# Who makes the low parts of the split weights: Pool's share moved to DVE in a Trainium2 expert-and-mixing kernel

## The chip, the core and the metric

The kernel runs on one core of one Trainium2 chip. The core has five queues of work: PE (the TensorE matmuls; its weight loads are listed apart as PEld), DVE (VectorE), ACT (ScalarE), POOL (GpSimd, called Pool here) and SP (SyncE, which issues transfers). The metric is the device time of the core in microseconds (us). Before the change it is 706.55 us, the median of three runs (706.11 to 706.99).

## The reference

Three layers follow one another on float32 arrays: a windowed attention, a mixture of experts in which each token goes to one of eight experts, and a gated mixing over the sequence (its weights come as float64).

```python
# attention: 4 batches, 8 heads, 576 tokens, 64 dims; plain or dilated window mask
attn = softmax(where(mask, q @ k.T / 8, -1e9));  x = attn @ v          # -> (4, 576, 512)
# experts: e = argmax of the token's logits, or the expert of the token before
h = np.maximum(x[b, s] @ w1[e], 0.0)                                    # w1[e]: 512 x 1024
out[b, s] = p[e] * (h @ w2[e])                                          # w2[e]: 1024 x 512
# gated mixing
h = np.maximum(x @ w_in, 0.0);  u, v = halves of h
gated = u * (w_spatial @ normalised(v) + b_spatial)
y = gated @ w_out
```

## The kernel before

**Split products.** A float32 product of the expert and mixing stages is made of three TensorE products of operands in the fp32r format: high by high, high by low, low by high. So every operand is split. `split` (line 548) first has ACT copy the source into the high part (line 549) and then another engine subtract the high part from the source, which gives the low part (line 550). Its last argument names that engine; without it, it is DVE.

**Experts.** After the attention (about the first 180 us of the trace) tokens of one expert are worked in blocks of 128 rows, block after block in one row. `block(j)` (line 1157) lets PE do the first layer of block j+1 (`stage1`, lines 999 to 1001, reading `w1h`, `w1l`, `xh`, `xl`), turn the rows of block j+2 (line 976), do the second layer of block j (`stage2`, lines 1033 to 1035, reading `w2h`, `w2l`, `hh`, `hl`), and turn the hidden rows of block j+1 (line 1012). In between, the next operands are made: `divide(1, j+2)` splits the w1 of block j+2 from the buffer `raw1` into `w1h`, `w1l` after stage 1 has read the old ones; `turn_x` makes `xh` (ACT, line 984) and `xl` (DVE, line 985); `divide(2, j+1)` splits w2 from `raw2`; `turn_h` makes `hh` (ACT, line 1022) and `hl` (DVE, line 1023). `divide` (line 950) works in four pieces of 128 x 1024; piece c = 1 is given to Pool, pieces 0, 2 and 3 to DVE. It runs under a condition, since consecutive blocks of one expert keep the weights; the tests and jumps of that condition have line 958.

**Mixing weights.** In twelve of the blocks `narrow` (line 1055) turns a piece of the float64 weights into float32 with five DVE steps (lines 1065 to 1071) and one of ACT, all in the buffer `scratch`. It returns the split of the result, which runs one block later (`rest.pop()()`, line 1192); that split gives the low part (`wil`, `wol`, 128 x 512) to Pool.

**Order.** Each engine takes its instructions in the order in which the code issues them. On DVE a block's order is: low parts of w1 if the expert changes, `xl`, low parts of w2 if the expert changes, `hl` twice, the five steps of `narrow`, and the copy of the next row list `ix` (line 970). On Pool it is: the gather of the rows of a later block (line 972, an indirect transfer), its piece of w1, its piece of the mixing weights, its piece of w2. SP fetches the next raw weights piece by piece (line 569) as soon as the piece in the buffer has been read.

Of the kernel before, what the change touches and what calls it, by code (L numbers as in the profile page):

```python
# [18 lines left out]
ET = mybir.EngineType  # L19
# [50 lines left out]
def moe_stack(ctx: ExitStack, tc: tile.TileContext, q, k, v, w_gate, w_local, w1, w2, w_in, w_sp, b_sp, w_out, out):  # L70
    nc = tc.nc
# [8 lines left out]

    # ---------------------------------------------------------------- constants
    warm = const.tile([128, 512], BF16, name="warm")
# [38 lines left out]

    # ---------------------------------------------------------------- routing state
    idxacc = rt.tile([128, NCOL], F32, name="idxacc")
    slot_i = rt.tile([128, LB], I32, name="slot_i")
    sel_all = rt.tile([128, LB, E], F32, name="sel_all")
    # of each token: its block among its expert's blocks, its row in it, and its weight
    trips = rt.tile([128, LB, 3], F32, name="trips")
# [7 lines left out]
    def steps(f):  # L135
        """A closure's parts, between which other work may come."""
        g = f()
        if g is not None:
            yield from g
# [9 lines left out]
    def router(b, xT, pieces, sides, bank):  # L149
        """Adds the closures that route batch b to stages."""  # L150
        st = {}
# [93 lines left out]
        def scan3():  # L245
            sv = st["sv"]
            if b == 0:
                # How many blocks of each expert hold tokens of the first batch.
                ci = rt2.tile([E, 2], I32, name="ci")
                nc.vector.tensor_scalar(out=ci[:, 0:1], in0=state["cum"], scalar1=127.0, scalar2=None, op0=ALU.add)  # L250
                nc.vector.tensor_scalar(out=ci[:, 1:2], in0=ci[:, 0:1], scalar1=7, scalar2=None, op0=ALU.arith_shift_right)
                state["first"] = rt.tile([E, 1], F32, name="first")
                nc.vector.tensor_copy(state["first"], ci[:, 1:2])
            nc.scalar.activation(sv[:, S:640], sv[:, 512:S].bitcast(F32), AF.Copy)
# [134 lines left out]
        def rows():  # L389
# [18 lines left out]
            if b < 3:  # L408
                return
            # The block before which every row of the first batch is there, if there is such a one.  # L410
            it = iota128[0:1, 0:n]
# [17 lines left out]
        def after():  # L429
            """Where this list's blocks of each expert begin, how many they are, and where the next list begins."""  # L430
            sf, en, nb, (j0, j1) = st["sf"], st["en"], st["nb"], LISTS[b]
            D = state["D"]
            base = rt2.tile([E, 1], F32, name="base")
            if b == 1:
                nc.vector.tensor_copy(base, sf)
            else:
                nc.vector.tensor_scalar(out=base, in0=sf, scalar1=state["got"], scalar2=float(j0), op0=ALU.subtract, op1=ALU.add)
            nc.vector.tensor_scalar(out=D[:, 2 * b - 2], in0=ident[0:E, 0:E], scalar1=base, scalar2=None, op0=ALU.mult)
            yield
            if b == 3:  # L440
                return
            n = j1 - j0
            tk = rt2.tile([E, 1], F32, name="tk")
            nc.vector.tensor_scalar(out=tk, in0=sf, scalar1=-1.0, scalar2=float(n), op0=ALU.mult, op1=ALU.add)
            yield
            nc.vector.tensor_scalar(out=tk, in0=tk, scalar1=0.0, scalar2=nb, op0=ALU.max, op1=ALU.min)
            yield
            got = rt.tile([E, 1], F32, name=f"got{b}")
            if b == 1:
                nc.vector.tensor_copy(got, tk)  # L450
            else:
                nc.vector.tensor_add(got, state["got"], tk)
            nc.vector.tensor_scalar(out=D[:, 2 * b - 1], in0=ident[0:E, 0:E], scalar1=got, scalar2=None, op0=ALU.mult)
            yield
            last = rt2.tile([E, 1], F32, name="last")
            nc.vector.tensor_scalar(out=last, in0=sf, scalar1=float(n), scalar2=None, op0=ALU.is_lt)
            yield
            l2 = rt2.tile([E, 1], F32, name="l2")
            nc.vector.tensor_scalar(out=l2, in0=en, scalar1=float(n), scalar2=None, op0=ALU.is_ge)
            yield  # L460
            nc.vector.tensor_mul(last, last, l2)
            yield
            st["last"], st["new"] = last, got
# [75 lines left out]
    stages = []  # L539
    state["bank"] = R()  # L540

    # ---------------------------------------------------------------- attention
    sc = ctx.enter_context(tc.tile_pool(name="sc", bufs=1))
# [11 lines left out]
    def fetch1(j, i):  # L555
        """The first two blocks have their own copies of w1, the first one also of w2, and use them as they are."""
        e = value(1, j, [ET.SP], E - 1)
# [24 lines left out]
    def attention(aw, ap, qkp, plan):  # L582
# [13 lines left out]
        npair = B * 4  # L596
        # A head's keys fill half of the rows and meet zeros in the other half, which lets the products use both heads' queries as they lie.
        kz = [[aw.tile([128, S], F32, name=f"kz{p}{hh}", bufs=1) for hh in range(2)] for p in range(2)]
# [4 lines left out]
        def load_qk(u):  # L603
            b, pr = divmod(u, 4)
            n, c = (96, 6) if pr < 2 else (72, 8)
            for w_, src in ((0, q), (1, k)):
                t = qkp.tile([96, 1024], F32, name=f"qk{w_}", bufs=3)
                if w_:
                    # Keys come head by head, each partition's tokens in one piece.
                    tv = t[0:n, 0:2 * c * D].rearrange("p (h m) -> p h m", h=2)  # L610
# [52 lines left out]
        def T_k(u, hh, tag="T"):  # L663
            """Turns a head's keys two neighbours at a time, whose dimensions then lie in the two halves of the rows."""
            def f():
# [172 lines left out]
        def feed(i):  # L838
            """Parts of the routing, as many as a step can take along; the tensor engine gets one only when its operands had time to be made."""
            nonlocal budget  # L840
# [83 lines left out]

    # ---------------------------------------------------------------- experts
    aps, aws, qks, w1s, mws, mps, xps = [ExitStack() for _ in range(7)]
# [23 lines left out]
    def divide(which, j, always=False):  # L950
        def parts():
            for c in range(4):
                split(*halves(which, c), nc.gpsimd if c == 1 else nc.vector)
        if always:
            parts()
            return
        ch = value(3, j, [ET.Activation, ET.DVE, ET.Pool], 1)
        with tc.If(ch > 0):  # L958
            parts()

    def own(key, pool, shape, dt, tag=None):
        """A tile that stays for all blocks."""
        if key not in P:
# [91 lines left out]
    def narrow(c):  # L1055
        """A piece of the float64 weights as float32, and that in two parts."""
        if c < 8:
# [13 lines left out]
        nc.vector.scalar_tensor_tensor(out=mf, in0=mf, scalar=2.0 ** -20, in1=sc.bitcast(F32), op0=ALU.mult, op1=ALU.mult)  # L1071
        return lambda: split(hi_, lo_, mf, nc.gpsimd)

    def early(kind, c=0):
        """The steps of blocks 0 and 1 that run beside the last of the attention."""
        def bankT():
# [22 lines left out]
    def pop(kind="any"):  # L1099
        """The next step of the routing; "pe": if the tensor engine has a part in it; "rest": all up to such a one."""  # L1100
        while stages and (kind == "any" or (kind == "pe") == hasattr(stages[0], "on_pe")):
# [4 lines left out]
    def ahead(what, j, must=False):  # L1106
        """Issues the gathers or fetches up to block j that the lists already give."""
        while done[what] <= min(j, NBLK - 1):
# [35 lines left out]
    def gate(j, engines=None):  # L1144
        """Blocks that every count of tokens fills run straight, the others where they hold any."""
        if j < SURE:
# [70 lines left out]
    rest = []  # L1217
# [9 lines left out]

    # ---------------------------------------------------------------- gated mixing over the sequence
    gr = ctx.enter_context(tc.tile_pool(name="gr", bufs=1, side="right", reuse_waits="tile"))
# [11 lines left out]
    def mixing(gw):  # L1241
# [17 lines left out]
        def turn_w(si):  # L1259
            """A part of the weights over the sequence, turned; the last 64 columns twice, for the two places of a batch's last tokens."""  # L1260
            w2x = G["w2x"]
# [61 lines left out]
        def norm3(g):  # L1323
            vr, _ = vn[g]
            if g % 9 == 4:
                # The last 64 tokens of two batches: a batch's high parts and, in the other half, its low parts.
                for t, a, z in ((tails[0], slice(0, 64), slice(64, 128)), (tails[1], slice(64, 128), slice(0, 64))):
# [59 lines left out]
        def project(b, gh, gl):  # L1387
# [3 lines left out]
            for ah, al, i in items:  # L1391
                o = gw.tile([128, C], F32, name="o", bufs=2)
                # The very last piece in two halves, so that less of it is left at the end.
                for cs in [slice(0, C)] if (b, i) != (B - 1, 3) else [slice(0, 256), slice(256, C)]:
# [86 lines left out]
```

## Time and profile before

| what | value |
|---|---|
| median of the runs | 706.55 us (706.11 to 706.99) |
| profiled execution: span from the first to the last instruction | 705.2 us |
| what the median has beside that span | 1.35 us |
| PE busy over the span | 672.2 us (95%) |
| DVE, ACT, POOL busy over the span | 423.9, 386.0, 194.2 us |

The median is 1.35 us above the profiled span; this is taken as what lies around the span. A PE that is listed as busy is not PE at its peak: a matmul's record is longer than the distance to the next one, since they are pipelined. What a row of the trace says is: start in us, length in us, engine, line, operation, the tile written <- the tiles read, shapes, how many merged, and in brackets the engine's idle time before it with what ended that idle time.

### The profile page before, as it was taken

How to read it: one execution, taken by the hardware profiler on the slowest of the kernel's cores; microseconds unless marked ns; L12 is line 12 of the kernel's file. 1: busy time of each engine (PE TensorE's matmuls, PEld its weight loads, DVE VectorE, ACT ScalarE, POOL GpSimd, SP SyncE). 2: the span in 40 equal slices, each digit the busy share in tenths (PEclk: the TensorE clock that was granted, in tenths of full speed). 3: DMA queues.
4: the chain of work that ended last, by engine and by line, in shares of the span. 5: the costliest groups of instructions: out<-in, count | busy, mean ns of one | idle time of the engine just before them, and what ended most of it. 6: DMA issues, size and time to landing. Idle time of an engine off the chain costs nothing. (4 is left out here: it accounts for less than half of the span.)

```text
span 705.2 us, 14287 instructions
## 1 busy us (share of the span) xinstructions
PE 672.2 (95%) x4395; PEld 571.1 (81%) x4396; DVE 423.9 (60%) x1379; ACT 386.0 (55%) x780; POOL 194.2 (28%) x226
## 2 busy tenths in 40 slices
PE   8999898989999999999999999897999999999998
PEld 6989797885478788787788877775898998998997
DVE  4667869777966747877866656342664164154151
ACT  5788777653635646666665556333735336335322
POOL 6443434341424405425424254112010110000000
PEclk9999999999999999999999999999999999999999
DMA  6776545594446776586556746415110220200102
GB/s 152 180 174 152 129 118 131 189 347 126 138 150 204 249 283 231 199 314 213 192 195 223 283 142 233 165 32 162 30 46 0 76 60 1 75 16 1 60 2 74
DMA packets 90644, 101.36 MB, mean 144 GB/s; under 512 B 49984, under 2 KB 60992, under 8 KB 90560
## 3 DMA queue, kind: packets, MB, share of 16 engines
q1 hardware_dynamic: 87120, 89.10, 39.7%
q0 software_dynamic: 3440, 11.27, 5.0%
q8 instruction: 36, 0.59, 0.3%
q14 instruction: 48, 0.39, 0.2%
HBM read 139.68 MB, written 17.30 MB: 223 GB/s over the span
## 5 line engine op out<-in xcount | busy, mean ns | idle before, releaser
L1001 PE MATMUL hp<-w1h,xl 128*128 128x512 f32 x168 | 66.9, 398 | 7.0 <-DVEq L958 6.1
L1033 PE MATMUL yp<-w2h,hh 128*128 128x512 f32 x176 | 71.6, 407 | 0.2 <-ACT hh L1022 0.2
L1035 PE MATMUL yp<-w2h,hl 128*128 128x512 f32 x176 | 69.9, 397 | 1.7 <-DVE hl L1023 1.7
L972 POOL DMA_INDIRECT xs<-x_d,ix x25 | 30.8, 1232 | 144.7 <-PE xTp L976 56.1
L1034 PE MATMUL yp<-w2l,hh 128*128 128x512 f32 x176 | 69.6, 395 | 0.0
L743 POOL TENSOR_TENSOR ms<-ms,mxa 96x384 f32<-96x384 f32 (+2 forms) x64 | 51.1, 799 | 64.9 <-DVE mxa L740 39.7
L999 PE MATMUL hp<-w1h,xh 128*128 128x512 f32 x168 | 68.4, 407 | 0.2 <-issue 0.2
L1000 PE MATMUL hp<-w1l,xh 128*128 128x512 f32 x168 | 66.4, 395 | 0.0
L740 DVE CUSTOM_DVE_ANT_0 ms<-S,masks 96x128 f32<-96x128 f32 (+2 forms) x224 | 54.4, 249 | 16.8 <-PE S L729 8.2
L550 DVE TENSOR_TENSOR w2l<-raw,w2h 128x1024 fp32r<-128x1024 f32 x30 | 48.7, 1649 | 24.5 <-ACT w2h L549 24.2
L550 DVE TENSOR_TENSOR w1l<-raw,w1h 128x1024 fp32r<-128x1024 f32 x30 | 55.7, 1902 | 5.3 <-ACT w1h L549 4.6
L729 PE MATMUL S<-kz,qT 128*96 128x128 f32 (+2 forms) x448 | 53.2, 259 | 0.4 <-POOL vt L632 0.4
L1151 POOL DMA_INDIRECT yg<-y_d,slot_i x14 | 13.4, 958 | 138.5 <-PE tr L1283 102.6
L776 PE MATMUL PV<-vt,ptS 128*96 128x65 f32 (+2 forms) x448 | 44.4, 240 | 7.0 <-issue 2.9
L1023 DVE TENSOR_TENSOR hl<-hTp,hh 128x512 fp32r<-128x512 f32 x44 | 30.3, 689 | 33.9 <-ACT hh L1022 31.9
L1022 ACT ACTIVATE hh<-hTp 128x512 fp32r<-128x512 f32 x44 | 26.2, 596 | 43.6 <-DVE hl L1023 38.2
L776 PEld LDWEIGHTS PV<-vt,ptS 128*96 128x96 f32 (+2 forms) x448 | 38.7, 156 | 9.7 <-issue 3.6
L729 PEld LDWEIGHTS S<-kz,qT 128*72 128x72 f32 (+1 forms) x448 | 45.4, 155 | 1.2 <-POOL vt L626 0.9
L1001 PEld LDWEIGHTS hp<-w1h,xl 128*128 128x128 f32 x168 | 31.5, 188 | 17.1 <-DVEq L958 8.4
L549 ACT ACTIVATE w2h<-raw 128x1024 fp32r<-128x1024 f32 x40 | 41.1, 1060 | 6.0 <-PE yp L1035 3.4
L549 ACT ACTIVATE gtiles<-gt 128x288 fp32r<-128x288 f32 (+2 forms) x48 | 15.7, 359 | 48.0 <-DVE gt L1377 48.0
L1035 PEld LDWEIGHTS yp<-w2h,hl 128*128 128x128 f32 x176 | 33.1, 188 | 10.7 <-DVE hl L1023 3.0
(309 smaller groups left out, 1825.5 us busy)
## 6 DMA issues: line engine op xcount, KB each, us to landing
raw<-in_moe_w SPq DMA_DIRECT2D x188, 512.0 KB
y_d<-y SPq DMA_DIRECT2D x30, 256.0 KB
qk<-in_q SPq DMA_DIRECT2D x32, 144.0 KB
qk<-in_k SPq DMA_DIRECT2D x32, 144.0 KB
x_d<-xo SPq DMA_DIRECT2D x32, 144.0 KB
scratch<-in_moe_w_in SPq DMA_DIRECT2D x8, 512.0 KB
out<-o SPq DMA_DIRECT2D x15, 256.0 KB
vt<-in_v SPq DMA_DIRECT2D x48, 64.0 KB
```

The lines of the kernel that those rows point to most:

```text
L549: nc.scalar.activation(dst_h, src, AF.Copy)
L550: (eng or nc.vector).tensor_tensor(out=dst_l, in0=src, in1=dst_h.bitcast(F32), op=ALU.subtract)
L729: nc.tensor.matmul(ps[0:nq, j, 0:nk], l, r, start=True, stop=True)
L740: nc.vector.tensor_tensor_reduce(out=ms[0:nq, j, 0:nk], in0=ps[0:nq, j, 0:nk], in1=masks[0:nq, m, 0:nk], scale=-0.125, scalar=3.0e38, op0= ...
L743: nc.gpsimd.tensor_tensor(out=ms[0:nq, 0:nb, 0:nk], in0=ms[0:nq, 0:nb, 0:nk], in1=mx[0:nq, 0:nb].unsqueeze(2).to_broadcast([nq, nb, nk]), ...
L776: nc.tensor.matmul(ops[0:nq, j], ptS[0:nk, j, 0:nq], r, start=True, stop=True)
L999: nc.tensor.matmul(ps[n], xh[:, kk], wh[:, kk, cs], start=(kk == 0), stop=False)
L1000: nc.tensor.matmul(ps[n], xh[:, kk], wl[:, kk, cs], start=False, stop=False)
L1001: nc.tensor.matmul(ps[n], xl[:, kk], wh[:, kk, cs], start=False, stop=(kk == 3))
L1033: nc.tensor.matmul(ps, hh[:, f], P["w2h"][:, f], start=(f == 0), stop=False)
L1034: nc.tensor.matmul(ps, hh[:, f], P["w2l"][:, f], start=False, stop=False)
L1035: nc.tensor.matmul(ps, hl[:, f], P["w2h"][:, f], start=False, stop=(f == 7))
```

## The change

The engine argument is gone from both calls, so DVE makes all low parts, and Pool drops out of the engines that read the condition of `divide`. Comments and docstrings were also dropped, which makes no instruction.

```diff
     def divide(which, j, always=False):
         def parts():
             for c in range(4):
-                split(*halves(which, c), nc.gpsimd if c == 1 else nc.vector)
+                split(*halves(which, c))
         if always:
             parts()
             return
-        ch = value(3, j, [ET.Activation, ET.DVE, ET.Pool], 1)
+        ch = value(3, j, [ET.Activation, ET.DVE], 1)
         with tc.If(ch > 0):
             parts()
...
-        return lambda: split(hi_, lo_, mf, nc.gpsimd)
+        return lambda: split(hi_, lo_, mf)
```

On DVE, at a block whose expert changes (`raw_3652` is the buffer of the raw w1), the difference of the two orders is:

```order
 L553 TENSOR_LOAD rowi
 L958 COMPARE_AND_BRANCH
-L550 TENSOR_TENSOR w1l<-raw_3652,w1h 128x1024 x3
+L550 TENSOR_TENSOR w1l<-raw_3652,w1h 128x1024 x4
 L958 UNCONDITIONAL_BRANCH x2
 L985 TENSOR_TENSOR xl<-xTp,xh 128x512
```

A fourth piece stands in DVE's row ahead of `xl`, between the same neighbours. The low part of a piece of the mixing weights stands on DVE after the change behind `xl` and ahead of the low parts of w2 (`raw_141` is the buffer of the raw w2):

```order
L550 TENSOR_TENSOR w1l<-raw_3652,w1h 128x1024 x4
L958 UNCONDITIONAL_BRANCH x2
L985 TENSOR_TENSOR xl<-xTp,xh 128x512
L550 TENSOR_TENSOR wil<-scratch,wih 128x512
L553 TENSOR_LOAD rowi
L958 COMPARE_AND_BRANCH
L550 TENSOR_TENSOR w2l<-raw_141,w2h 128x1024 x4
```

Before, `wil` was not in DVE's row, and the two splits had three pieces each. On Pool, in the same blocks, before the change (`xs_...` are the gathered rows, `ix_...` the row lists):

```order
L972 DMA xs_3097<-x_d,ix_2925 128x512
L553 TENSOR_LOAD rowi
L958 COMPARE_AND_BRANCH
L550 TENSOR_TENSOR w1l<-raw_3652,w1h 128x1024
L958 UNCONDITIONAL_BRANCH x2
L550 TENSOR_TENSOR wil<-scratch,wih 128x512
```

And after the change, from the same gather on:

```order
L972 DMA xs_3097<-x_d,ix_2925 128x512
L958 UNCONDITIONAL_BRANCH x2
L972 DMA xs_2927<-x_d,ix_3095 128x512
L958 UNCONDITIONAL_BRANCH x2
L972 DMA xs_3097<-x_d,ix_3687 128x512
```

Pool's row there holds only the gathers and the jumps.

## Rows read from the trace of the kernel before

**Rows 1.** The page: the span.
```profile
span 705.2 us, 14287 instructions
```
**Rows 2.** Busy time by stretch: experts, then mixing; last three: PEclk, DMA share, GB/s.
```profile
180.00:476.00 296.00, 285.98 (x1347) 225.87 (x1345) 197.18 (x274) 165.26 (x241) 106.79 (x69) 1.00 0.57 201
476.00:705.20 229.20, 221.78 (x1375) 202.05 (x1373) 95.03 (x246) 94.72 (x243) 14.58 (x16) 1.00 0.15 47
```
**Rows 3.** Groups by line, 180 to 476 us: busy, mean ns, idle before, releasers.
```profile
L1035 PE MATMUL yp<-w2h,hl 128*128 128x512 f32 x176 | 69.9, 397 | 1.7 <-DVE hl L1023 1.7
...
L1001 PE MATMUL hp<-w1h,xl 128*128 128x512 f32 x168 | 66.9, 398 | 7.0 <-DVEq L958 6.1 <-DVE xl L985 0.9
...
L550 DVE TENSOR_TENSOR w1l<-raw,w1h 128x1024 fp32r<-128x1024 f32 x30 | 55.7, 1902 | 5.3 <-ACT w1h L549 4.6 <-DMA y_d<-y 0.7
L550 DVE TENSOR_TENSOR w2l<-raw,w2h 128x1024 fp32r<-128x1024 f32 x29 | 47.4, 1663 | 24.5 <-ACT w2h L549 24.2 <-DVE xl L985 0.2
...
L550 POOL TENSOR_TENSOR w1l<-raw,w1h 128x1024 fp32r<-128x1024 f32 x10 | 25.7, 2571 | 0.2
```
**Rows 4.** Timeline of PE around the wait at 297 us.
```profile
296.49 0.40 PE L1000 MATMUL hp<-w1l,xh 128*128 128x512 f32 x1
297.89 0.50 PE L1001 MATMUL hp<-w1h,xl 128*128 128x512 f32 x1 [1.00 <-DVEq L958]
298.22 0.40 PE L999 MATMUL hp<-w1h,xh 128*128 128x512 f32 x1
298.46 0.40 PE L1000 MATMUL hp<-w1l,xh 128*128 128x512 f32 x1
```
**Rows 5.** Timeline of PE: the first matmul after other such waits.
```profile
234.07 0.50 PE L1001 MATMUL hp<-w1h,xl 128*128 128x512 f32 x1 [0.90 <-DVE xl L985]
...
433.86 0.50 PE L1035 MATMUL yp<-w2h,hl 128*128 128x512 f32 x1 [0.85 <-DVE hl L1023]
...
443.19 0.50 PE L1001 MATMUL hp<-w1h,xl 128*128 128x512 f32 x1 [2.16 <-DVEq L958]
...
462.82 0.50 PE L1035 MATMUL yp<-w2h,hl 128*128 128x512 f32 x1 [0.82 <-DVE hl L1023]
```
**Rows 6.** Timeline of DVE, 291 to 298 us (the x3 row and its third piece).
```profile
291.53 5.71 DVE L550 TENSOR_TENSOR w1l<-raw,w1h 128x1024 fp32r<-128x1024 f32 x3 [0.42 <-ACT w1h L549]
...
293.81 3.43 DVE L550 TENSOR_TENSOR w1l<-raw,w1h 128x1024 fp32r<-128x1024 f32 x1
297.16 0.68 DVE L985 TENSOR_TENSOR xl<-xTp,xh 128x512 fp32r<-128x512 f32 x1
```
**Rows 7.** Timeline of POOL over the same stretch.
```profile
291.85 1.75 POOL L972 DMA_INDIRECT xs<-x_d,ix  x1 [7.91 <-PE yp L1035]
293.62 2.54 POOL L550 TENSOR_TENSOR w1l<-raw,w1h 128x1024 fp32r<-128x1024 f32 x1
296.12 2.25 POOL L550 TENSOR_TENSOR wil<-scratch,wih 128x512 fp32r<-128x512 f32 x1
```
**Rows 8.** Timeline of ACT over the same stretch.
```profile
289.22 3.91 ACT L549 ACTIVATE w1h<-raw 128x1024 fp32r<-128x1024 f32 x4
...
293.99 0.59 ACT L984 ACTIVATE xh<-xTp 128x512 fp32r<-128x512 f32 x1
```
**Rows 9.** Timeline of DVE at 188 us, where POOL has no work.
```profile
188.18 3.50 DVE L550 TENSOR_TENSOR w1l<-raw,w1h 128x1024 fp32r<-128x1024 f32 x3
```
**Rows 10.** Timeline of DVE before the waits at 433 and 443 us.
```profile
429.39 3.82 DVE L550 TENSOR_TENSOR w2l<-raw,w2h 128x1024 fp32r<-128x1024 f32 x2 [0.68 <-ACT w2h L549]
...
435.84 1.22 DVE L550 TENSOR_TENSOR w1l<-raw,w1h 128x1024 fp32r<-128x1024 f32 x1 [0.45 <-ACT w1h L549]
437.56 4.97 DVE L550 TENSOR_TENSOR w1l<-raw,w1h 128x1024 fp32r<-128x1024 f32 x2 [0.50 <-ACT w1h L549]
```
**Rows 11.** Timeline of PE: the turn of the rows gathered at 291.85 us.
```profile
303.13 0.60 PE L976 MATMUL xTp<-ident,xs 128*128 128x128 f32 x4
```
**Rows 12.** The tile of gathered rows: time from issue to landing.
```profile
DMA to landing us min/median/max: 3.4/4.2/6.6
```

## The prediction

> **What bounds the kernel now.** I read the stretches first: where is PE not busy, and at which clock does it run? From 180 us on, the granted clock is 1.00 (the upper of the two levels, 2.4 GHz), in the expert stage as in the mixing stage [rows 2]. In the expert stage PE is listed busy for 285.98 of 296.00 us, DVE for 197.18 and POOL for 106.79; in the mixing stage POOL has 14.58 us of work in all. So the change can act in the expert stage only, and there PE is the bound, apart from about 10 us.
>
> Next come the groups by line of that stage. The reader is to look at the idle time in front of each PE group. Two groups carry nearly all of it: line 1001, which needs `xl`, waits 7.0 us, and line 1035, which needs `hl`, waits 1.7 us; both waits are ended by DVE [rows 3]. Where the releaser is called DVEq L958, it is the jump at the end of the condition around the split: `xl` comes right behind it. These 8.7 us are eight waits: one is shown in full [rows 4], four more by the matmul that ends them [rows 5], and three repeat the first at 324.16, 350.43 and 414.20 us with 0.97, 0.98 and 0.97 us of idle time. A matmul's record is 0.40 us long while the next starts 0.24 us later (298.22 to 298.46), and here 1.40 us lie between 296.49 and 297.89 [rows 4]. A wait therefore costs its idle time plus 0.16 us: 8.65 + 8 x 0.16 = 9.9 us in all.
>
> Last, the timelines of DVE, POOL and ACT in front of one such wait, to see why DVE is late. DVE needs 5.71 us for three pieces of w1, from 291.53 to 297.24; its third piece alone is on record for 3.43 us from 293.81 on [rows 6]. At 188 us, where POOL has nothing to do, three such pieces take 3.50 us [rows 9]. It isn't ACT that holds DVE up: ACT has all four high parts done at 289.22 + 3.91 = 293.13 us, before DVE begins its third piece [rows 8]. POOL is at its own piece from 293.62 to 296.16 [rows 7], and DVE's third piece ends 1.08 us behind that, which is about the time of one piece alone. Then POOL's piece of `wil` begins at 296.12 and needs 2.25 us, to 298.37, that is 1.13 us past the end of DVE's piece. The two engines take turns, a whole instruction at a time; while POOL is at its piece, DVE stands still.
>
> The page SBUF — State Buffer of the Trainium skill says so as a rule (section "SBUF: two separate sides"): VectorE and GpSimd have a pair of ports in common, an exclusive lock for a whole instruction, and a VectorE operation with two SBUF inputs contends for it with a GpSimd operation that reads SBUF. By that rule a piece given to POOL saves DVE nothing. This case's trace agrees (3.43 us for the piece in POOL's way).
>
> **The change part by part.**
>
> *A piece on DVE.* From rows 9 with one record of 1.22 us [rows 10]: (3.50 - 1.22) / 2 = 1.14 us from piece to piece, so four take 3.50 + 1.14 = 4.64 us. POOL needs 2.57 us for one on average [rows 3].
>
> *The w1 splits ahead of a wait.* Where DVE works through without a gap, as at 291.53, three pieces in POOL's way took 5.71 us and four alone take 4.64: `xl` comes 1.07 us earlier. Four waits are of this kind, costing 1.16, 1.13, 1.14 and 1.13 us, so each keeps at most 0.1 us: 4.2 us are gained. The w2 splits one block earlier become shorter too, so DVE may start these sooner and the rest goes as well: 4.5 us; I take 4.35.
>
> At 437.56 two pieces take 4.97 us behind an idle 0.50 us [rows 10]. Alone, two take 3.50 - 1.14 = 2.36; the new piece fills the gap and adds 1.14 - 0.50 = 0.64. So `xl` comes 4.97 - 2.36 - 0.64 = 1.97 us earlier, of a wait of 2.16 + 0.16 = 2.32 us: 1.97 gained, 0.35 left. The wait that ends at 234.07 has the same pattern ahead of it and costs 1.06 us: all gained.
>
> *The w2 splits ahead of a wait.* At 429.39 two pieces take 3.82 us behind a gap of 0.68 us [rows 10]: 3.82 - 2.36 - (1.14 - 0.68) = 1.00 us earlier, against 0.85 + 0.16 = 1.01. The one at 462.82 is alike (0.82 + 0.16 = 0.98). Gained: 1.98 us.
>
> *The other splits.* Of 20 splits 12 have no wait behind them. They change DVE's queue alone, and in the same direction, since 30 pieces of w1 took 55.7 us [rows 3] while 40 alone take some 40 x 1.14 = 46 us. No gain on PE is counted for them.
>
> *The mixing weights.* DVE gets twelve pieces of 128 x 512. Nearest row: `xl`, of the same size, 0.68 us [rows 6]. They stand behind `xl`, so PE's next need of `xl` isn't touched; behind them wait the low parts of w2 and `hl`, which DVE now reaches about 1 us earlier anyway. I take 0 for them; if that cover were gone at each of the twelve, 12 x 0.68 = 8.2 us would be the upper end. The operand `mf` was read by POOL and is now read by DVE itself, so the next step of `narrow` waits for nobody.
>
> *What leaves POOL.* Its tests of the condition, one per split, with no wait of PE behind them: 0. POOL's gathers no longer queue behind splits. SP fetches the next raw piece when the piece before is read; piece 1 is now read by DVE as its second and not by POOL at 296.16 us [rows 7], so transfers start earlier, on queues that are busy 0.57 of the time [rows 2]: 0.
>
> Sum: 4.35 + 1.97 + 1.06 + 1.98 = 9.4 us. The span goes from 705.2 [rows 1] to 695.8 us; the median of the runs lies 1.35 us above the span, so 706.55 - 9.4 = 697.1 us.
>
> **The rivals.**
>
> *DVE becomes the bound (slower).* DVE is the engine PE waits for, and it gets 32 instructions more. If the 3.43 us were not POOL's doing, but came from something that stays, each split would take one piece longer, 1.14 us. The place is the row w1 pieces, `xl`, line 1001 (and w2 pieces, `hl`, line 1035); each of the eight waits would grow by 1.14: 9.1 us, 715.7 us, and up to 8.2 more if `wil` got into the way too. It decides from the point on which a fourth piece costs more than the stretch that goes, 5.71 - 3.50 = 2.21 us. For it: only one row shows three pieces without POOL. Against: DVE and POOL end one behind the other twice within 3 us [rows 6, 7]. 5%.
>
> *The gathers starve.* The gather at 291.85 stays on POOL for 1.75 us beside DVE's pieces [rows 7]; it may be held up by them, as POOL's `wil` is. With four pieces in a row and POOL shut out until the last, at 291.53 + 4.64 = 296.17, the rows would land by 296.17 + 6.6 = 302.8 us at worst [rows 12]; PE turned them at 303.13 [rows 11], and would do so 1.16 us earlier, at 301.97. That makes up to 0.8 us at each of ten w1 splits, 8 us given back: 705 us. Against: the gather did end at 293.60 in the middle of DVE's row of pieces, and the median landing is 4.2 us [rows 12]. 4%. [...]
>
> *Half of it.* PE, once it no longer waits for `xl`, meets something else close behind: `xh` of ACT (done at 294.58, against a need of `xl` at 296.7, [rows 8]), a raw piece that lands late, or the twelve new instructions ahead of `hl`. Then 3 to 7 us stay, 699.5 to 703.5 us. For it: most of these waits are only 1 us, so a small delay elsewhere eats much of one. Against: 2 us of room on ACT. 15%.
>
> *Nothing moves.* The gaps are hidden by a wait later in the stage, up to the last block, whose y rows the mixing stage gathers. Against: the mixing stage begins with PE's own last products, which move along. 706.5 us, 4%.
>
> **How the numbers follow.** The forecast, 8.5 to 10.3 us gained (696.2 to 698.1), has 72%: the upper end takes all 9.9 us of waits and some 0.4 of a run's spread. Of the rivals 28% are left, half of it in the partial gain. The range 695.8 to 703 holds the forecast and nearly all of the partial one, some 85%. A difference of 0.2%, 1.4 us, is about what a measurement of this kernel can tell from none. Faster: 72 + 15 + most of the gathers' case = 90%; same: 4%; slower: 6%.
>
> **What would show it.** POOL with no split in the expert stage; the w1 pieces of DVE at 1.2 us each with none above 2 us, 40 of them in less than the 55.7 us that 30 took; the waits in front of line 1001 at about 0.3 to 0.8 us in all and those of line 1035 gone. It is wrong if the pieces of DVE stay long without POOL, if the waits are back with another releaser (a transfer, ACT), or if line 976 begins to wait for `xs`.

## The result, and the profile after

The changed kernel takes 695.46 us (median of four runs, 694.24 to 699.27), the kernel before in the same comparison 706.77 us (706.11 to 710.61). The ratio is 0.9839, 95% interval 0.9803 to 0.9874. Forecast were 697.1 us and a range of 695.8 to 703.0: the direction, the place and the mechanism hold, the gain is larger than forecast, and the time lies 0.3 us below the range.

The profiled execution is shorter by 705.2 - 694.2 = 11.0 us. First the page's span and, from the busy times by stretch, the expert stage and what follows it (length; then PE, PEld, DVE, ACT, POOL; then granted clock, DMA share, GB/s). These lines answer to [rows 1, 2]:

```profile
span 694.2 us, 14124 instructions
```
```profile
180.00:465.00 285.00, 283.12 (x1345) 226.19 (x1344) 192.47 (x303) 164.46 (x240) 34.81 (x37) 1.00 0.59 208
465.00:694.20 229.20, 222.62 (x1376) 203.60 (x1374) 95.56 (x246) 94.63 (x243) 14.56 (x16) 0.99 0.15 46
```

The stretches are cut where the last product of line 1035 starts, to a whole us (475.94 us before, 465.20 after). In the first of them PE is idle for 1.9 us in place of 10.0. From that last product to the end of the span there are 229.3 us before and 229.0 after (705.2 - 475.94 and 694.2 - 465.20). DVE is busy for 192.47 us in the first stretch, less than the 197.18 before, although it does 29 instructions more there; POOL falls from 106.79 to 34.81 us.

The groups by line of the same stretch (busy, mean ns, idle before, releasers) answer to [rows 3]:

```profile
L1033 PE MATMUL yp<-w2h,hh 128*128 128x512 f32 x176 | 71.7, 407 | 0.5 <-ACT hh L1022 0.5
...
L1035 PE MATMUL yp<-w2h,hl 128*128 128x512 f32 x175 | 69.4, 397 | 0.0
L1001 PE MATMUL hp<-w1h,xl 128*128 128x512 f32 x168 | 66.5, 396 | 0.1
L550 DVE TENSOR_TENSOR w1l<-raw,w1h 128x1024 fp32r<-128x1024 f32 x40 | 46.4, 1223 | 4.1 <-ACT w1h L549 3.3 <-DMA y_d<-y 0.8
L550 DVE TENSOR_TENSOR w2l<-raw,w2h 128x1024 fp32r<-128x1024 f32 x38 | 45.7, 1224 | 14.8 <-ACT w2h L549 14.5 <-DMA raw<-in_moe_w 0.2
```

Forty pieces of w1 take 46.4 us where thirty took 55.7, and no piece is long any more. In the view of line 550 (instructions by operation, ns min/median/max) the spread of the forty is:

```profile
L550 DVE TENSOR_TENSOR w1l<-raw,w1h x40: 1211/1220/1325, 185.5 to 431.4; 128x1024 fp32r<-128x1024 f32 x40
```

The same block as in [rows 4, 6, 7], on DVE, POOL and PE:

```profile
289.00 4.63 DVE L550 TENSOR_TENSOR w1l<-raw,w1h 128x1024 fp32r<-128x1024 f32 x4 [0.42 <-ACT w1h L549]
293.55 0.68 DVE L985 TENSOR_TENSOR xl<-xTp,xh 128x512 fp32r<-128x512 f32 x1
294.15 0.68 DVE L550 TENSOR_TENSOR wil<-scratch,wih 128x512 fp32r<-128x512 f32 x1
```
```profile
289.32 1.73 POOL L972 DMA_INDIRECT xs<-x_d,ix  x1 [12.21 <-DVE ix L970]
```
```profile
294.70 0.40 PE L1000 MATMUL hp<-w1l,xh 128*128 128x512 f32 x1
294.94 0.39 PE L1001 MATMUL hp<-w1h,xl 128*128 128x512 f32 x1
295.17 0.40 PE L999 MATMUL hp<-w1h,xh 128*128 128x512 f32 x1
```

Four pieces need 4.63 us (4.64 forecast), `xl` is done at 294.23, 0.7 us ahead of PE, and PE starts a product every 0.24 us. Of the eight waits one is left, where 0.35 us were forecast to stay [rows 5, 10]: 0.50 us between two starts, 0.27 more than usual.

```profile
432.73 0.40 PE L1000 MATMUL hp<-w1l,xh 128*128 128x512 f32 x1
433.23 0.50 PE L1001 MATMUL hp<-w1h,xl 128*128 128x512 f32 x1
433.56 0.39 PE L999 MATMUL hp<-w1h,xh 128*128 128x512 f32 x1
```

The gathers land as they did before. In the first profile of the kernel before, only 3 of the 25 gathers have a landing on record, and [rows 12] is made of these three. With all 25 on record the same view reads, in the changed kernel and in a second profile of the kernel before (`before_again`, below):

```profile
DMA to landing us min/median/max: 3.3/5.6/8.0
```
```profile
DMA to landing us min/median/max: 3.4/5.4/7.7
```

PE waits for a gather once in this stage, ahead of the first turn of rows, for 0.72 us before and 0.84 us after.

### The profile page after: what moved, and what is told of

It reads as the page before. It is cut to its first block, busy times and chain, and to the rows that moved or that the text cites. A ratio compares the mean times of both kernels' runs of the same rounds, so it can differ in the third digit from the quotient of the medians.

```text
span 694.2 us, 14124 instructions
## 1 busy us (share of the span) xinstructions
PE 669.7 (96%) x4395; PEld 571.9 (82%) x4396; DVE 420.4 (61%) x1411; ACT 385.3 (56%) x780; POOL 122.8 (18%) x194
## 5 line engine op out<-in xcount | busy, mean ns | idle before, releaser
L550 DVE TENSOR_TENSOR w1l<-raw,w1h 128x1024 fp32r<-128x1024 f32 x40 | 46.4, 1223 | 4.1 <-ACT w1h L549 3.3
L549 ACT ACTIVATE w1h<-raw 128x1024 fp32r<-128x1024 f32 x40 | 39.3, 1048 | 1.8 <-ACT w1h L549 1.0
L1033 PEld LDWEIGHTS yp<-w2h,hh 128*128 128x128 f32 x176 | 33.2, 188 | 7.5 <-ACT hh L1022 0.7
```

The lines of the kernel that those rows point to most:

```text
L549: nc.scalar.activation(dst_h, src, AF.Copy)
L550: (eng or nc.vector).tensor_tensor(out=dst_l, in0=src, in1=dst_h.bitcast(F32), op=ALU.subtract)
L1033: nc.tensor.matmul(ps, hh[:, f], P["w2h"][:, f], start=(f == 0), stop=False)
```

## The experiments

The figure compared below is the length of the expert stage, from PE's first turn of rows at about 183 us (line 976) to the start of its last product of line 1035. It takes out what the attention and the mixing differ by from run to run. Before: 475.94 - 183.68 = 292.26 us; after: 465.20 - 183.06 = 282.14 us; gain 10.1 us. The first and the last line before, then after:

```profile
183.68 0.66 PE L976 MATMUL xTp<-ident,xs 128*128 128x128 f32 x4 [0.72 <-DMA xs<-x_d,ix]
...
475.94 0.40 PE L1035 MATMUL yp<-w2h,hl 128*128 128x512 f32 x1
```
```profile
183.06 0.66 PE L976 MATMUL xTp<-ident,xs 128*128 128x128 f32 x4 [0.84 <-DMA xs<-x_d,ix]
...
465.20 0.40 PE L1035 MATMUL yp<-w2h,hl 128*128 128x512 f32 x1
```

The cost of a wait is given here as the distance between the starts of the two products around it, less the usual 0.235 us.

**Both kernels once more** (no edit).

> The changed kernel once more, for the size of the gain and the spread of its runs. Theory A (the eight waits of the expert stage are gone, each was dearer than its idle time plus 0.16 us; the rest of the 11 us is what differs from run to run in the stretches at the lower clock): 10 us of the gain lie between PE's turn of rows at 183 us and the last product of the expert stage in every profile, and the total scatters by some us with the granted clock (0.990 to 0.997); ratio 0.983 to 0.988. Theory B (part of the gain is made in the attention, 0.6 us before 183 us, by the changed kernel): that 0.6 us is there again.

Measured: 695.58 us (seven runs, 694.21 to 698.81), ratio 0.9813 (0.9783 to 0.9842), a little below the 0.983 to 0.988 expected. Expert stage 282.13 us. PE's first turn of rows comes at 186.27 us, in place of 183.06: theory B fell, the 0.6 us of the first pair are scatter.

> The kernel before, profiled a second time. Theory A: the eight waits stand at the same places with the same length within 0.1 us, the expert stage takes 292.3 us from the turn of rows at 183 us to its last product, and the stretches at the lower clock lie elsewhere than at 120 and 150 us, so the attention ends up to 0.7 us earlier or later. Theory B: the attention ends at the same time as in the first profile within 0.1 us.

Measured: 705.51 us (one run); expert stage 292.61 us, with the same eight waits (1.08, 1.13, 1.14, 1.13, 1.12, 0.98, 2.31, 0.98 us); first turn of rows at 182.40 us, with the lower clock at 82 and 122 us in place of 120 and 152. As theory A has it.

**The two halves of the change apart.** First the experts' weights alone (from the changed kernel):

```diff
-        return lambda: split(hi_, lo_, mf)
+        return lambda: split(hi_, lo_, mf, nc.gpsimd)
```

> The experts' weights wholly on DVE, the low parts of the mixing weights left on POOL. Theory A (the gain comes from the w1 and w2 pieces; POOL's piece of the mixing weights runs beside xl and hl, which have one SBUF operand, and keeps DVE from nothing that PE waits for): 695.5 us, within 0.7 us of the changed kernel; the w1 pieces at 1.2 us, the first w2 piece of a block up to 0.3 us longer. Rival (moving the mixing weights was part of the gain): 697 to 699 us.

Then the mixing weights alone (from the kernel before):

```diff
-        return lambda: split(hi_, lo_, mf, nc.gpsimd)
+        return lambda: split(hi_, lo_, mf)
```

> The other half alone: the mixing weights' low parts on DVE, POOL keeps its piece of the experts' weights. Theory A: the eight waits stay, 706.8 us within 0.7 us; DVE's w1 rows stay at 5.7 us for three pieces. Rival (what counts is how much work is on DVE): 0.68 us later at each of twelve blocks, up to 712 us. Rival (POOL's piece of the mixing weights was in the way): 702 us.

Measured: 697.34 us, ratio 0.9839 (0.9807 to 0.9871), expert stage 282.25 us; and 708.5 us, ratio 0.9996 (0.9967 to 1.0025), expert stage 292.28 us. Line 1001 in the groups by line, of the first and of the second:

```profile
L1001 PE MATMUL hp<-w1h,xl 128*128 128x512 f32 x168 | 66.5, 396 | 0.1
```
```profile
L1001 PE MATMUL hp<-w1h,xl 128*128 128x512 f32 x168 | 67.0, 399 | 7.0 <-DVE xl L985 4.8 <-DVEq L958 2.1
```

The whole gain of the expert stage comes from the experts' pieces. The mixing weights neither cost nor bring anything there. The second median is 1.7 us above the 706.8 expected, but the kernel before had 708.51 in the same comparison. The first median is 1.8 us above the changed kernel's, more than the 0.7 expected; the intervals overlap and the expert stage doesn't show it. About 0.25 of the 1.8 us lies outside the span: a run's time less its own span is 1.71 us in the kernel before and in the changed kernel (the 1.35 us of the section on time and profile set one span against the median of other runs), and 1.96 us here. Whether the rest is more than scatter stays open.

**One layer at a time.** `nc.gpsimd` for piece 1 of w2 only, and of w1 only (and POOL among the readers of the condition there):

```diff
-                split(*halves(which, c))
+                split(*halves(which, c), nc.gpsimd if which == 2 and c == 1 else nc.vector)
```

> DVE makes all four pieces of w1 (and the mixing weights), POOL keeps its piece of w2. Theory A (each wait hangs on the split right ahead of it): the six waits for xl go as in the changed kernel, the two for hl stay with about 1 us each; expert stage 282.1 + 2.2 = 284.3 us, time 2.2 us above the changed kernel, near 697.8 us. Rival (only the total of DVE's and POOL's work counts): halfway between both kernels, 701 us.

> DVE makes all four pieces of w2 (and the mixing weights), POOL keeps its piece of w1. Theory A: the two waits for hl go; the wait of 1.05 us near 234 us and the one of 2.3 us near 443 us stay; the four of 1.14 us get shorter by the 0.6 us by which the w2 split of the block before ends sooner. Expert stage about 287.7 us, time near 701.2 us. Rival (the w1 rows alone set the six waits): all six stay, expert stage 290 us, 703.5 us.

Measured: 700.78 us, ratio 0.991 (0.988 to 0.994), expert stage 286.37 us; and 704.83 us, ratio 0.9949 (0.9913 to 0.9985), expert stage 289.45 us. Idle time in the groups by line, of the first and of the second:

```profile
L1035 PE MATMUL yp<-w2h,hl 128*128 128x512 f32 x176 | 69.9, 397 | 1.7 <-DVE hl L1023 1.7
L1001 PE MATMUL hp<-w1h,xl 128*128 128x512 f32 x168 | 67.0, 399 | 1.3 <-DVE wr L361 0.7 <-DVE xl L985 0.5
```
```profile
L1035 PE MATMUL yp<-w2h,hl 128*128 128x512 f32 x176 | 69.8, 396 | 0.0
L1001 PE MATMUL hp<-w1h,xl 128*128 128x512 f32 x168 | 67.7, 403 | 4.8 <-DVE xl L985 2.7 <-DVEq L958 2.1
```

With w1 on DVE the waits for `hl` stay (0.98 and 1.00 us); with w2 on DVE they go, the waits of 1.05 and 2.31 us for `xl` stay, and the four of 1.14 become 0.43, 0.78, 0.44 and 0.78. So a shorter w2 split does let the next w1 split begin sooner. The expert stages come out 2.1 and 1.8 us above their numbers (284.3 and 287.7), the times 3.0 and 3.6 us above theirs (697.8 and 701.2). In the first, waits appear that I hadn't counted: 0.85 us at 198, 0.40 at 327 and at 415 us, of splits that start late behind a w2 split with POOL in it; besides, a run's time less its span is 2.6 us there in place of 1.7, for a reason that stays open. In the second, the clock falls inside the stage, behind the wait at 442 us (below).

**POOL's work without its data.** The changed kernel, with an instruction on POOL on which nobody waits: once reading and writing SBUF, once two that only write. `extra` holds from the fourth block on; POOL is again among the readers of the condition in both. The two edits in one, cut:

```diff
                 split(*halves(which, c))
+                if extra and c == 1:
...
+                    nc.gpsimd.tensor_tensor(out=dum, in0=dum, in1=dum, op=ALU.subtract)   # pool_reads
+                    nc.gpsimd.memset(dum, 1.0)                                            # pool_writes, twice
...
```

> The changed kernel, with a useless instruction added on POOL at every split from the fourth block on: a subtraction of 128 x 720 from a tile of its own into itself (SBUF in, SBUF out), some 1.8 us, on which nobody waits. Theory A (the two engines exclude each other): in each w1 split one of DVE's four pieces is on record for 2.5 to 3 us, xl comes 1.8 us later, most waits for xl are back with 0.5 to 2 us; expert stage 288 to 291 us, time 702 to 705 us. Rival (DVE's long pieces came from waiting for POOL's data or from the condition's jumps): pieces of 1.2 us, 695.6 us.

> The changed kernel, with two useless instructions on POOL at the same places: memsets of 128 x 720 on a tile of its own, which write SBUF and read nothing, together about as long as the subtraction. The page SBUF - State Buffer of the Trainium skill (SBUF: two separate sides) says that a DVE operation with two SBUF inputs is excluded only by a GpSimd operation that reads SBUF. By that rule: pieces of 1.2 us, expert stage 282.1 us, time 695.6 us within 0.7 us. Rival (any work on POOL is in the way): pieces of 1.9 us and more, expert stage 285 us and more, 698 to 701 us.

Measured: 700.26 us, ratio 0.99 (0.987 to 0.9931), expert stage 286.65 us, five waits for `xl` of 0.59, 0.59, 0.65, 0.86 and 1.45 us; and 695.88 us, ratio 0.9827 (0.9798 to 0.9855), expert stage 282.13 us, one wait of 0.23 us. The w1 split near 290 us with the reading instruction, on DVE and on POOL:

```profile
288.01 5.82 DVE L550 TENSOR_TENSOR w1l<-raw,w1h 128x1024 fp32r<-128x1024 f32 x4 [0.41 <-ACT w1h L549]
```
```profile
290.09 1.53 POOL L956 TENSOR_TENSOR dum<-dum 128x720 f32<-128x720 f32 x1
```

And with the two writing ones:

```profile
289.92 4.63 DVE L550 TENSOR_TENSOR w1l<-raw,w1h 128x1024 fp32r<-128x1024 f32 x4 [0.42 <-ACT w1h L549]
```
```profile
291.98 0.72 POOL L956 MEMSET dum<- 128x720 f32 x1
292.75 0.70 POOL L957 MEMSET dum<- 128x720 f32 x1
```

This shows the cause. An instruction of 1.53 us that shares no data with DVE makes its four pieces 1.19 us longer, and five of the six waits for `xl` are there, while 1.42 us of writing in the middle of them costs DVE nothing. As POOL reads the condition in both, that part of the change brings nothing either. The size was set too high (1.8 us for an instruction that took 1.53, so a stage of 288 to 291 us in place of 286.65 and 702 to 705 us in place of 700.3).

By the Trainium skill, page SBUF — State Buffer (section "SBUF: two separate sides"), a VectorE operation with two SBUF inputs contends only with a GpSimd operation that reads SBUF. The two traces agree (1.19 us longer with the reading instruction, 0.00 with the writing ones); but the subtraction and the memset differ in kind too, so that the reading is what counts isn't shown by itself.

**The fourth piece's own cost.**

```diff
-                split(*halves(which, c))
+                if c != 1 or always:
+                    split(*halves(which, c))
+                else:
+                    h_, _, s_ = halves(which, c)
+                    nc.scalar.activation(h_, s_, AF.Copy)
```

> The changed kernel without the low part of piece 1 in the conditional splits (18 of 20; the high part is still made, and the products read the low part of an older split): DVE has three pieces again and POOL none, so the fourth piece's own cost is seen. Theory A (POOL's piece cost DVE 2.2 us where DVE's own costs 1.14 us, and after the change one wait of 0.27 us is left): w1 rows of 3.5 us, the last wait gone, expert stage 281.9 us, time 0.3 us under the changed kernel, the same for the measurement. Rival (DVE's amount of work still sets the pace): 1.14 us at each of several blocks, 2 to 9 us under the changed kernel.

Measured: 695.78 us, ratio 0.9831 (0.9782 to 0.9879), expert stage 281.93 us, and no wait for `xl` left (the products of line 1001, four lines further down in this kernel):

```profile
L1005 PE MATMUL hp<-w1h,xl 128*128 128x512 f32 x168 | 66.3, 395 | 0.0
```

DVE's fourth piece costs PE 0.2 us in all.

**Where the runs of the kernel before lose more** (no edits).

> The kernel before, profiled once more, to see where its runs lose time beside the eight waits. Theory A (lower-clock stretches fall anywhere, mostly in the attention, in both kernels alike): expert stage 292.3 us, none in it. Theory C (a wait of PE in the expert stage is sometimes followed by a stretch at the lower level of the clock, which a kernel without waits can't have): a stretch at half clock inside the expert stage or at the start of the mixing, expert stage 1 to 2 us longer.

> The same as before_c2, a further sample. Theory A: expert stage 292.3 us. Theory C: in one of the two samples it is 1 to 2 us longer, with a lower-clock stretch behind a wait.

> The changed kernel, a further sample: expert stage 282.1 us under both theories, with no lower-clock stretch from 183 us to its end; what its span has above or below 694 us lies in the attention and in the first 30 us of the mixing, where the lower clock falls.

Measured: 708.22, 707.6 and 696.82 us, with expert stages of 294.50, 293.94 and 282.75 us. Theory C holds in one of the two samples, the other shows a second cause. In the first, ACT's copies and so DVE's pieces start with gaps, and the split near 265 us becomes a ninth wait, of 1.84 us; in the first profile `xl` was there in time in this block. Why ACT came late stays open. DVE in that stretch, then PE's first product behind the wait:

```profile
264.58 1.23 DVE L550 TENSOR_TENSOR w1l<-raw,w1h 128x1024 fp32r<-128x1024 f32 x1 [0.54 <-issue]
266.80 5.59 DVE L550 TENSOR_TENSOR w1l<-raw,w1h 128x1024 fp32r<-128x1024 f32 x2 [0.99 <-ACT w1h L549]
272.31 0.68 DVE L985 TENSOR_TENSOR xl<-xTp,xh 128x512 fp32r<-128x512 f32 x1
```
```profile
273.05 0.50 PE L1001 MATMUL hp<-w1h,xl 128*128 128x512 f32 x1 [1.68 <-DVEq L958]
```

In the second, PE's products come 0.43 us apart for 3.4 us, close behind its longest wait, at a granted clock of 0.81 over these 6 us (timeline of PE, then busy times by stretch as above):

```profile
442.50 0.50 PE L1001 MATMUL hp<-w1h,xl 128*128 128x512 f32 x1 [2.15 <-DVEq L958]
...
444.27 0.63 PE L1001 MATMUL hp<-w1h,xl 128*128 128x512 f32 x1
444.69 0.63 PE L999 MATMUL hp<-w1h,xh 128*128 128x512 f32 x1
```
```profile
440.00:446.00 6.00, 3.85 (x13) 2.72 (x12) 3.98 (x6) 1.19 (x2) 0.00 (x0) 0.81 0.20 65
```

The same stood in the kernel with w2 alone on DVE, behind the same wait. The expected 282.1 us of the third run came out 0.6 us longer, with a wait of 0.51 us for `hl` at 427 us, where the w2 split started later.

Expert stages of all profiles, in us:

| POOL has pieces of the experts' weights as before | POOL has none |
|---|---|
| 292.26, 292.61, 294.50, 293.94 (kernel before) | 282.14, 282.13, 282.75 (changed kernel) |
| 292.28 (mixing weights moved) | 282.25 (mixing weights left), 282.13 (POOL writes), 281.93 (three pieces) |

## Why the prediction was right or wrong

**Right: what bounds, and where the change acts.** PE's waits for `xl` and `hl` carried the gain. They went at the places named, and next to nothing took their place: 0.3 us more of waiting for ACT's `hh` (below), nothing for a transfer, nothing for the gathers. The prediction's bound on the gathers, 6.6 us to landing, rested on three of them and was too low (7.7 us in the second profile of the kernel before); the rival fell all the same, since the landings didn't move.

**Right: the mechanism.** The reading of [rows 6, 7, 9], that DVE stood still for POOL's piece, rested on one stretch without POOL. The kernel with the useless reading instruction shows it without any exchange of data. The rival "DVE becomes the bound" fell with the three pieces: 0.2 us for the fourth.

**Right: the piece and the order.** 4.63 us for four pieces against 4.64, and 0 for the mixing weights: their pieces took 0.68 us each, as `xl` did, and the two halves apart gave nothing for them in the expert stage.

**Wrong: the sum, 9.4 us where the expert stage gained 10.1.** The failing step is what a wait costs: "its idle time plus 0.16 us". It left out the restart. After a wait the next product starts 0.33 us behind the first (297.89 to 298.22, in [rows 4] itself) and not 0.24, so each wait costs 0.1 us more (the eight 10.8 us by their starts, and not 9.9): 0.7 for the seven that went. Next, "each keeps at most 0.1 us" for the four waits of 1.14 us: none of it stayed, 0.2 us more than the 4.35 taken, because the w2 split one block earlier ends sooner; w2 alone on DVE shows that step by itself. The wait at 443 us kept 0.27 and not 0.35. Against these stands 0.3 us more of waiting of line 1033 for `hh`: 0.5 us in the groups by line after, and before

```profile
L1033 PE MATMUL yp<-w2h,hh 128*128 128x512 f32 x176 | 71.6, 407 | 0.2 <-ACT hh L1022 0.2
```

9.4 + 0.7 + 0.2 + 0.1 - 0.3 = 10.1.

**Wrong: the range.** Its lower end allowed "some 0.4 of a run's spread". The runs of one kernel scatter over 5 us and more (the kernel before from 705.07 to 715.25), with granted clocks of 0.983 to 0.998 in the kernel before and, in the profiles, stretches of half clock, mostly in the attention, whose place and number differ. The first three runs, 0.9 us apart, said nothing of that. The remaining 0.9 us of the first pair of profiles are of this kind: 0.6 in the attention, where both kernels' further profiles lie from 182.4 to 186.3 us, and 0.3 behind the experts.

**Not foreseen: the kernel before is the less steady one.** The waits of 1 to 2 us were read from one profile. In two of four profiles of that kernel the expert stage was 2.2 and 1.7 us longer still, for a ninth wait and for a stretch at the lower clock. This may be part of why the later comparisons gave more (ratio 0.9813 and, for POOL only writing, 0.9827) than the 10.1 us of the expert stage, 0.986, would; it isn't shown, since most of those runs have no profile.

## What to carry to other kernels

A piece of work that DVE gives to POOL to save time can cost DVE more than the piece itself, when both read two operands from SBUF (here 2.2 us against 1.14): compare the length of DVE's instruction beside POOL's with one where POOL is idle, before counting POOL as help. Price a wait of TensorE by the distance between the starts of products on both sides of it, down to where the usual distance is back, not by the idle time alone. And a range needs the scatter of many runs: three that agree within 1 us can be followed by some that are 5 us away.

## What the runs showed of the hardware that was not expected

- POOL's indirect gathers, which read the row list `ix`, wait for DVE's piece in return, and for one piece only: in the changed kernel the eight that begin while a piece of the experts' weights is under way take 1.73 to 1.87 us on POOL and end 0.8 to 0.9 us behind that piece, the next piece notwithstanding. One that begins 0.04 us ahead of a piece, at 263.50 us, takes 0.95 us; in the kernel before, one that begins while `xl` is under way, at 370.63 us, takes 0.96. They don't land later for it: in the changed kernel the gather of 289.32 us, held up, landed 4.0 us after its issue, that of 276.17, not held up, after 6.65.
- TensorE's clock fell to its lower level (products 0.43 us apart) for 3.4 us close behind a wait of 2.15 us in two profiles, and not behind the same wait in four others. In the first profile of the changed kernel it fell behind the first long wait of the mixing stage, at 481 us, after 2.34 us of idle time that DVE's `yg` ended; in its second profile, behind 2.22 us of idle time at the same place, it didn't:

```profile
481.30 0.63 PE L1295 MATMUL mm<-wih,x2h 128*128 128x512 f32 x1
481.72 0.63 PE L1296 MATMUL mm<-wil,x2h 128*128 128x512 f32 x1
```

What decides whether it falls stays open.
